# Two attention tiles kept in an empty weight buffer, and one attention tile and one operand sum moved to a later place

## The chip, the core and the metric

The kernel runs on one core of one Trainium2 chip. A core has five engines with a program of their own each: PE (TensorE) multiplies matrices into PSUM banks, DVE (VectorE) and ACT (ScalarE) work element by element, POOL (GpSimd) does the same out of SBUF only, and SP issues DMA transfers in the order of its own queue. An engine takes its instructions strictly in order, so a waiting instruction holds all that stand behind it. The metric is the device time of one execution in microseconds (us): the median of three runs is 307.73 us.

## The reference, cut to what matters

The first half is a linear attention (8 batches, 8 heads, 576 positions, 64 numbers per head), the second a gated feed-forward layer over all 4608 rows.

```python
r = np.maximum(x, 0.0)                     # phi, for q and k
phi = concatenate([r * cos, r * sin])      # 128 numbers per head and position
kv  = einsum('bhsf,bhsd->bhfd', k_p, v);  z = sum(k_p)
x   = (q_p @ kv) / (q_p @ z + 1e-6)        # per head; rows become (4608, 512)
out = (gelu(x @ w_gate) * (x @ w_val)) @ w_out    # d_ff = 1536
```

## The kernel before, in words

**Two ways of cutting the rows.** Attention goes by batch: batch b has five tiles of 128 rows (t = 0 to 4; of tile 4 only the last 64 rows are new). The feed-forward layer goes by block: nine blocks of 512 rows. Batch 2 begins at row 1152, so its tile 3 (rows 1536 to 1663) and its tile 4 (1664 to 1727) are the first 192 columns of block 3. Batch 3's tiles 0 and 1 and half of tile 2 are the rest of block 3; the other half of tile 2, tile 3 and tile 4 belong to block 4.

**One attention tile** (`nm_unit`, L310): eight small matmuls on PE (L312, 65 columns each) fill two PSUM banks, 6 and 7 unless told otherwise; DVE adds the epsilon (L323, `den`), takes the reciprocal (L324, `rec`) and multiplies (L325) into a tile `x_sb` in SBUF. The pool of `x_sb` has four buffers (`xsp`, L54), handed out in turn. Later `turn_x` (L376) has SP issue a transposing DMA per piece (L379) from `x_sb` into `xT` of the block; a buffer of `x_sb` can be written again once the DMAs that read it have landed.

**One block of the feed-forward layer.** Units 0 to 11 each make 128 of the 1536 columns. `gv_unit` (L421) makes one unit with plain matmuls (L431), a Gelu on ACT (L440, into one of two `gel` buffers) and a product on DVE (L443, into `hT`). From block 2 on some units are made in pairs by a seven-product scheme for two-by-two matrices (class `Pair`, L644; matmuls L655), which needs sums of weights, of `xT` (`x_sum`, L623, on POOL, into `fs`) and, for the output product, of `hT` (`h_sum`, L520, into `sm`, DVE or POOL). The helpers of a pair are p1 (copy L674 on ACT), p5 (copy L678), p6 (add L682 on DVE), p2 (Gelu L687), p3 (Gelu L691), p7 (add L695, product L696 on DVE) and p4 (product L700 on DVE). `product` (L539, matmuls L548, adds L561, copies L566) makes the output of the block before.

**Order.** Nothing is scheduled automatically: the order of the calls is the order of each engine's program. Block 2 (`block2`, L1017) makes half units 8 to 11, unit 4, pair (0, 1), unit 5, pair (2, 3), unit 6 and unit 7; `rest(jt)`, called once for each place jt, holds what else is done there: the attention of batch 3 (dictionary `tiles`, L1021; `turn_x` one place later), the products and sums of block 1 (`o_step`), the scaling of q and k of batch 4 (`early`, L1012, ACT and POOL), loads, and casts of v. Block 2's unit 7 puts its value half into bank 6 (L1065). From block 3 on `step` (L705) calls `numerators` (L1080) for the attention: at the start of a block it stands between p1 and p5 of the first pair, and there takes tile 4 of batch n. Its guard `b > 3` leaves out batch 3, whose tile 4 is in block 2's `tiles`. `kv_unit` of batch n + 1 (L265, matmuls L271) writes banks 6 and 7 in the next place but one.

**The empty place.** `wx` (L108) holds the sums S1, S2 and S4 of the weight columns 1024 to 1279, [128, 3, 2, 256] bf16. They are computed on POOL in block 3 (L1100, `w_sum`); up to there nothing reads or writes `wx`. One third of it is as large as one `x_sb` tile.

**The sum.** `SUMS` (L901) says at which place which sum of `hT` is made. For block 2's `o_step`, entry `9: "8"` is S4 of block 1's second half, a DVE instruction (L530, 128x768 bf16); product 3, which reads it, comes at place 11.

Of the kernel before, what the change touches and what calls it, by code (L numbers as in the profile page):

```python
# [10 lines left out]
BF16 = mybir.dt.bfloat16  # L11
# [5 lines left out]
def kernel(  # L17
# [15 lines left out]
    B, H, S, D = q.shape  # L33
# [20 lines left out]
    xsp = ctx.enter_context(tc.tile_pool(name="xsp", bufs=4))  # L54
# [11 lines left out]
    def bank(i):  # L66
        return ps[:, i]
# [40 lines left out]
    wx = weights.tile([128, 3, CT // 2, WX - WJ], BF16)  # L108
# [99 lines left out]
    def cast_v(b, m0, m1, copy, j0=0, j1=R):  # L208
        copy(  # L209
            vx[:, m0:m1, j0:j1, 0:D],  # L210
            staged["v", b][:, m0:m1, j0 * D:j1 * D].rearrange("p m (j d) -> p m j d", d=D),
        )
# [8 lines left out]
    def turn_q(b):  # L221
        for i in range(2):
            nc.sync.dma_start_transpose(
                out=qt_tile(b)[:, i].rearrange("f m (j p) -> f (m j) p", p=64),
                in_=phi["q", b][64 * i:64 * i + 64].rearrange("p m j f -> p (m j f)"),
            )

    def q_cols(b, t, h):
        c0 = min(t * 128, S - 128)
        return qT[b][:, h % 2, h // 2, c0:c0 + 128]  # L230
# [34 lines left out]
    def kv_unit(b):  # L265
        kp = phi["k", b]
        for m in range(NP):
            for j in range(R):
                for i in range(2):
                    rr = slice(64 * i, 64 * i + 64)  # L270
                    nc.tensor.matmul(  # L271
                        bank(6 + i)[:, m * (D + 1):(m + 1) * (D + 1)],
                        lhsT=kp[rr, m, j, :],
                        rhs=vx[rr, m, j, :],
                        start=(j == 0),
                        stop=(j == R - 1),
                    )
        kv_sb[b] = attn2.tile([128, NP, 2, D + 1], BF16, name="kv_sb")
        for i in range(2):
            nc.scalar.copy(  # L280
                kv_sb[b][:, :, i, :],
                bank(6 + i)[:, 0:NP * (D + 1)].rearrange("p (m d) -> p m d", m=NP),
            )
# [26 lines left out]
    def nm_unit(b, t, b0=6):  # L310
        for h in range(H):
            nc.tensor.matmul(  # L312
                bank(b0 + h // 4)[:, (h % 4) * (D + 1):(h % 4 + 1) * (D + 1)],
                lhsT=q_cols(b, t, h),
                rhs=kv_sb[b][:, h // 2, h % 2, :],
                start=True,
                stop=True,
            )
        nm = ps[:, b0:b0 + 2, 0:4 * (D + 1)].rearrange("p g (h d) -> p g h d", h=4)
        den = attn2.tile([128, 2, 4], FP32, name="den")  # L320
        rec = attn2.tile([128, 2, 4], FP32, name="rec")
        x = xsp.tile([128, 2, 4, D], BF16, name="x_sb")
        nc.vector.tensor_scalar_add(den, nm[:, :, :, D], EPS)  # L323
        nc.vector.reciprocal(rec, den)  # L324
        nc.vector.tensor_tensor(  # L325
            x,
            nm[:, :, :, 0:D],
            rec[:, :, :, None].to_broadcast([128, 2, 4, D]),
            op=ALU.mult,
        )  # L330
        xs[b, t] = x.rearrange("p g h d -> p (g h d)")
# [44 lines left out]
    def turn_x(b, t):  # L376
        x = xs.pop((b, t))
        for blk, c, o, m in pieces(b, t):
            nc.sync.dma_start_transpose(  # L379
                out=xT_block(blk)[:, :, c:c + m], in_=x[o:o + m, :]  # L380
            )
# [241 lines left out]
    def x_sum(n, i, eng=nc.gpsimd):  # L623
        if n not in xb:
            xt = xT[n]
            own = fs[:, (1 - n % 2) * 2 * BLK:(2 - n % 2) * 2 * BLK].bitcast(BF16)
            xb[n] = {
                "B11": xt[:, 0:CP, 0:256], "B12": xt[:, 0:CP, 256:512],
                "B21": xt[:, CP:CT, 0:256], "B22": xt[:, CP:CT, 256:512],
                "T": own.rearrange("p (i c n) -> p i c n", i=4, c=CP),  # L630
            }
        b = xb[n]
        x, y = (("B12", "B11"), ("B22", "T1"), ("B22", "B12"), ("B21", "T2"))[i]
        b[f"T{i + 1}"] = b["T"][:, i]
        eng.tensor_tensor(b[f"T{i + 1}"], b[x], b[y], op=ALU.subtract)  # L635
# [166 lines left out]
    prep("q", 0, 0, (6, 7))  # L802
    dummies(1, 1)
    nm_unit(0, 2, 4)
    turn_x_pe(0, 1, 7, act_copy)
    turn_j(0, 0, 2, (6, 7), 2, act_copy)
    turn_j(0, 2, 4, (6, 7), 3, dve_copy)
    gv_tile(0)
    nm_unit(0, 3, 6)
    gv_done(0)  # L810
    turn_x_pe(0, 2, 4, act_copy)
# [74 lines left out]
    def js(a, b):  # L886
# [12 lines left out]
        (5, 0): [(7, "q", 5, R), (7, "k", 5, R), (7, "v")],  # L899
    }  # L900
    SUMS = {  # L901
        2: {0: "1", 1: "2", 2: "34", 3: "567", 9: "8"},
        8: {i: str(i + 1) for i in range(8)},
    }
    for n in range(3, 8):
# [13 lines left out]
    def more(n, jt):  # L919
        for what in MORE.get((n, jt), ()):  # L920
            if len(what) == 3:
                w_sum(*what, eng=nc.gpsimd)
            else:
                x_sum(*what)
# [5 lines left out]
    def o_step(n, jt):  # L930
        p, u = divmod(jt, 6)
        for i in ((1, 2), (5,), (6,), (7,), (4,), (3,))[u]:
            product(n - 1, p, i, ps[:, 4, 0:CH], ps[:, 5, 0:CH], ps[:, 4, CH:C])
        for i in map(int, SUMS[n].get(jt, "")):
            eng = nc.gpsimd if n > 2 or jt == 3 else nc.vector
            h_sum(n - 1, i // 5, f"S{(i - 1) % 4 + 1}", eng=eng)
        if jt % 3 == 1:
            flush()

    def start_loads(n, jt):  # L940
        for b, name, *part in LOADS.get((n, jt), ()):
            if len(part) == 1:
                load(nc.sync, name, b, part[0], part[0] + 2)
            elif part:
                load(nc.sync, name, b, 0, NP, *part)
            else:
                for m in (0, 2):
                    load(nc.sync, name, b, m, m + 2)

    def scale(b, name, sines_, cosines):  # L950
        for j in sines_:
            prep(name, b, 1, (j,), eng=nc.scalar)
        for j in cosines:
            prep(name, b, 0, (j,))
# [57 lines left out]
    def early(jt):  # L1012
        for what in EARLY.get(jt, "").split():
            part = "cs".index(what[0])
            prep_both(4, part, int(what[1]), nc.scalar if part or jt > 8 else nc.gpsimd)

    def block2():  # L1017
        b, n = 3, 2
        o_step(n, 0)

        tiles = {4: 0, 5: 1, 6: 2, 7: 3, 10: 4}  # L1021

        def rest(jt):
            if jt - 1 in tiles:
                turn_x(b, tiles[jt - 1])
            if 0 < jt < JT - 1:
                o_step(n, jt)
            if jt in tiles:
                nm_unit(b, tiles[jt])
            if jt + JT in SCALE:  # L1030
                scale(*SCALE[jt + JT])
            if jt in (1, 2):
                cast_v(b, 2 * jt - 2, 2 * jt, act_copy)
            if jt == 3:
                kv_unit(b)
            early(jt)
            if jt == 1:
                turn_x(2, 3)
                turn_x(2, 4)
            start_loads(n, jt)  # L1040
            if jt == 2:
                for i in range(4):
                    x_sum(n, i)
            more(n, jt)
            if jt in (9, 10):
                m = 2 * (jt - 9)
                cast_v(4, m, m + 2, nc.gpsimd.tensor_copy)

        def rests(*jts):
            return [lambda jt=jt: rest(jt) for jt in jts]  # L1050

        turn[0] = 1
        for jt in range(4):
            for i in range(2):
                half, unit = divmod(2 * jt + i, 4)
                gv_unit(n, unit + 8, half * HALF, HALF)
                if jt == i == 0:
                    nm_unit(2, 4)
                    turn_q(3)
            rest(jt)  # L1060
        gv_unit(n, 4, to=(2, 3))
        rest(4)
        step(Pair(n, 0, 0, 2, range(5, 8)), None, *rests(5, 6, 7), std=5, to=1)
        step(Pair(n, 1, 2, 0, range(8, 11)), None, *rests(8, 9, 10), std=6, to=1)
        gv_unit(n, 7, to=(0, 6))  # L1065
        rest(11)
# [13 lines left out]
    def numerators(n, jt):  # L1080
        b, t = n + 1, {6: 0, 8: 1, 10: 2, 11: 3, 0: 4}.get(jt)
        if jt == 0:
            b = n
        if t is not None and b > 3:
            nm_unit(b, t)
            turns.append((b, t))

# [44 lines left out]
    turn[0] = 1  # L1132
    block1()
    block2()

    old, places = None, (0, 1, 2)
    for n in range(3, NB):
        jt = 0
        for T in range(JT // 2):
# [7 lines left out]
            jt = jts.stop  # L1147
# [17 lines left out]
    for what in (  # L1165
# [3 lines left out]
        if isinstance(what, str):  # L1169
            p = "ST".index(what[0])  # L1170
# [33 lines left out]
```

## Time and profile before

| | us |
|---|---|
| median of three runs (lowest, highest) | 307.73 (307.56, 307.85) |
| the profiled execution's own time | 307.25 |
| its span, first to last instruction | 305.5 |
| around the span | 1.75 |
| PE busy, of the span | 294.7 (96%) |
| DVE, ACT, POOL busy | 227.8, 203.9, 175.3 |
| granted clock of PE, mean | 0.997 |

The profile comes from one execution. Its times count from the first instruction. "Idle before, releaser" is the time in which the engine waited ahead of an instruction and what ended that wait. The starts of one group of matmuls and the next tell how fast PE goes: it starts a new group while the results of the last are still on their way, so a group's own duration is longer than the step to the next.

### The profile page before, as it was taken

What the parts mean: (1) busy time and instruction counts of PE and PEld (TensorE: products, weight loads), DVE (VectorE), ACT (ScalarE), POOL (GpSimd) and SP (SyncE); (2) the same over time, 40 slices, a digit from 0 to 9 for tenths busy, and PEclk for the clock granted to TensorE, in tenths of its full rate; (3) what the DMA queues carried; (4) which work ended last, traced back from release to release, by engine and by line L of the source; (5) the groups of instructions that cost most, each with busy time, mean ns of one, the idle gap of its engine ahead of it and who ended that gap; (6) DMA issues with size and microseconds to landing.
All of it is one profiled execution on the core that took longest, in us unless ns stands there. A gap on an engine that the chain in (4) does not pass through costs nothing.

```text
span 305.5 us, 8095 instructions
## 1 busy us (share of the span) xinstructions
PE 294.7 (96%) x3113; PEld 231.2 (76%) x3131; DVE 227.8 (75%) x497; ACT 203.9 (67%) x403; POOL 175.3 (57%) x147
## 2 busy tenths in 40 slices
PE   7899999999999899999999999999999999999993
PEld 2574455745788658888888888888898988888882
DVE  5866995998976675779677967796678785766782
ACT  7865593997574688869586958695655556555630
POOL 6675450000029999955955595669935965397310
PEclk9999999999999999999999999999999999999998
DMA  7999999989799997998999699918832321303045
GB/s 271 252 178 220 337 293 394 298 164 226 164 185 225 247 314 154 187 281 235 127 167 344 199 138 220 281 30 138 135 67 54 69 46 34 71 3 70 2 86 121
DMA packets 73175, 53.68 MB, mean 176 GB/s; under 512 B 45392, under 2 KB 62544, under 8 KB 73136
## 3 DMA queue, kind: packets, MB, share of 16 engines
q1 hardware_dynamic: 63360, 41.17, 59.2%
q0 software_dynamic: 9696, 11.93, 17.0%
q8 instruction: 24, 0.39, 0.6%
q14 instruction: 15, 0.12, 0.2%
q10 hardware_dynamic: 80, 0.07, 0.1%
HBM read 37.75 MB, written 9.44 MB: 154 GB/s over the span
## 4 chain that ended last, share of the span: by engine, by line
PE 75%; DMA 7%; issue 6%; DVE 5%; ACT 4%; POOL 1%; SPq 0%; POOLq 0%; DVEq 0%; ACTq 0%
PE ps L655 32%; PE ps L548 19%; PE ps L431 13%; PE ps L464 3%; DMA xT<-x_sb 3%; PE ps L271 2%; DMA st<-in_v_dram 2%; PE ps L312 2%; DMA wv_sb<-in_moe_w_val_dram 2%; DVE hT L443 1%; ACT gel L440 1%; POOL st L530 1%; ACT phis L178 1%; PE ps L402 1%; DVE x_sb L325 1%
## 5 line engine op out<-in xcount | busy, mean ns | idle before, releaser
L530 POOL TENSOR_TENSOR sm<-hT 128x768 bf16<-128x768 bf16 x26 | 42.7, 1643 | 17.7 <-PE ps L655 8.0
L635 POOL TENSOR_TENSOR fs<-xT 128x512 bf16<-128x512 bf16 x14 | 16.2, 1155 | 56.8 <-ACT vx L209 43.6
L655 PE MATMUL ps<-fs,ws 128*128 128x256 bf16 x312 | 44.4, 273 | 0.0
L655 PEld LDWEIGHTS <-ws 128*128 128x128 bf16 x416 | 39.5, 98 | 5.7 <-ACT ps L674 0.3
L695 DVE TENSOR_TENSOR ps<-fs,ps 128x512 f32<-128x512 f32 x35 | 24.3, 695 | 24.9 <-PE ps L655 23.1
L655 PE MATMUL ps<-xT,wg_sb 128*128 128x256 bf16 x280 | 42.0, 272 | 0.2 <-ACT gel L440 0.2
L431 PE MATMUL ps<-xT,wv_sb 128*128 128x512 bf16 (+1 forms) x167 | 37.9, 348 | 0.1
L431 PE MATMUL ps<-xT,wg_sb 128*128 128x512 bf16 (+1 forms) x155 | 36.8, 346 | 0.7
L548 PEld LDWEIGHTS <-sm 128*128 128x128 bf16 x336 | 32.3, 98 | 3.8
L687 ACT ACTIVATE gel<-ps 128x512 f32<-128x512 f32 x35 | 20.8, 594 | 19.5 <-PE ps L655 19.5
L561 DVE TENSOR_TENSOR o_sb<-sm,ps 128x256 f32<-128x256 f32 x56 | 23.4, 418 | 11.6 <-ACT sm L566 9.7
L655 PEld LDWEIGHTS <-wg_sb 128*128 128x128 bf16 x280 | 27.3, 98 | 5.5 <-issue 0.5
L678 ACT COPY fs<-ps 128x512 f32<-128x512 f32 x35 | 20.6, 588 | 16.2 <-DVE ps L695 16.2
L443 DVE TENSOR_TENSOR hT<-gel,ps 128x512 bf16<-128x512 f32 (+1 forms) x42 | 25.3, 606 | 8.1 <-PE ps L431 5.6
L440 ACT ACTIVATE gel<-ps 128x512 f32<-128x512 f32 (+1 forms) x42 | 22.3, 538 | 13.1 <-PE ps L431 10.7
L548 PEld LDWEIGHTS <-hT 128*128 128x128 bf16 x288 | 28.0, 98 | 3.8 <-issue 0.2
L325 DVE TENSOR_TENSOR x_sb<-ps,rec 128x512 bf16<-128x512 f32 x38 | 26.3, 691 | 3.0 <-DMA xT<-x_sb 1.5
L696 DVE TENSOR_TENSOR hT<-gel,ps 128x512 bf16<-128x512 f32 x35 | 24.1, 687 | 3.3
L691 ACT ACTIVATE gel<-ps 128x512 f32<-128x512 f32 x35 | 21.0, 599 | 8.2 <-PE ps L655 6.9
L431 PEld LDWEIGHTS <-wv_sb 128*128 128x128 bf16 x168 | 16.3, 98 | 12.9 <-issue 0.3
L530 POOL TENSOR_TENSOR sm<-hT,sm 128x768 bf16<-128x768 bf16 x12 | 19.7, 1644 | 11.0 <-PE ps L548 11.0
L192 ACT ACTIVATE phis<-st,sin_t 128x512 bf16<-128x512 f32 x36 | 25.6, 721 | 0.0
(134 smaller groups left out, 636.2 us busy)
## 6 DMA issues: line engine op xcount, KB each, us to landing
out_dram<-o_sb SPq DMA_DIRECT2D x69, 128.0 KB, 2.5
st<-in_v_dram SPq DMA_DIRECT2D x10, 576.0 KB, 6.7
st<-in_q_dram SPq DMA_DIRECT2D x5, 640.0 KB, 5.5
st<-in_q_dram SPq DMA_DIRECT2D x5, 512.0 KB, 5.0
st<-in_k_dram SPq DMA_DIRECT2D x4, 640.0 KB, 6.1
st<-in_k_dram SPq DMA_DIRECT2D x4, 576.0 KB, 4.6
st<-in_q_dram POOLq DMA_DIRECT2D x4, 576.0 KB, 12.1
st<-in_k_dram SPq DMA_DIRECT2D x4, 512.0 KB, 5.4
```

Source lines behind the costliest of these rows:

```text
L192: nc.scalar.activation(o, i, AF.Relu, scale=tab[:, j:j + 1])
L325: nc.vector.tensor_tensor(x, nm[:, :, :, 0:D], rec[:, :, :, None].to_broadcast([128, 2, 4, D]), op=ALU.mult,)
L431: nc.tensor.matmul(bank(to[g])[:, 0:w], lhsT=wt[:, ct, js], rhs=xt[:, ct, c0:c0 + w], start=(ct == 0), stop=(ct == CT - 1),)
L440: nc.scalar.activation(gel[:, 0:w], bank(to[0])[:, 0:w], AF.Gelu)
L443: nc.vector.tensor_mul(hT[n][:, jt, c0:c0 + w], gel[:, 0:w], bank(to[1])[:, 0:w])
L530: eng.tensor_tensor(a[name][:, j0:j1], a[x][:, j0:j1], a[y][:, j0:j1], op=op)
L548: nc.tensor.matmul(at, lhsT=hs.setdefault(key, h_parts(n, p))[a][:, j], rhs=ts[b][:, j], start=(j == 0 and i in ((1, 2, 4, 5), (1, 4, 5))[ ...
L561: nc.vector.tensor_tensor(o, got[key, k], x, op=op)
L655: nc.tensor.matmul(to[:, 256 * half:256 * half + 256], lhsT=w_part(a, j * 128, (j + 1) * 128)[:, ct], rhs=xb[self.n][b][:, ct], start=(hal ...
L691: nc.scalar.activation(gel1, bank(MIX), AF.Gelu)
L695: nc.vector.tensor_tensor(bank(val), self.m5, self.sum, op=ALU.add)
L696: nc.vector.tensor_tensor(self.h(1), both(gel1), both(bank(val)), op=ALU.mult)
```

## The change

Three edits. The tiles 3 and 4 of batch 2 are written to the first two thirds of `wx` instead of two `x_sb` buffers, and transposed from there; so the order in which buffers of `x_sb` are handed out skips these two. Tile 4 of batch 3 leaves block 2 (place 10) and is attended by `numerators` at the start of block 3, as the later batches' tile 4 is; its `turn_x` follows in the same place of block 3. Sum S4 of block 1's second half is made at place 10 instead of 9. The changed file has three lines more, so later lines stand 3 higher there.

```diff
         den = attn2.tile([128, 2, 4], FP32, name="den")
         rec = attn2.tile([128, 2, 4], FP32, name="rec")
-        x = xsp.tile([128, 2, 4, D], BF16, name="x_sb")
+        if (b, t) in ((2, 3), (2, 4)):
+            x = wx[:, t - 3].rearrange("p c (h d) -> p c h d", d=D)
+        else:
+            x = xsp.tile([128, 2, 4, D], BF16, name="x_sb")
...
-        2: {0: "1", 1: "2", 2: "34", 3: "567", 9: "8"},
+        2: {0: "1", 1: "2", 2: "34", 3: "567", 10: "8"},
...
-        tiles = {4: 0, 5: 1, 6: 2, 7: 3, 10: 4}
+        tiles = {4: 0, 5: 1, 6: 2, 7: 3}
...
         if jt == 0:
             b = n
-        if t is not None and b > 3:
+        if t is not None and b > 3 - (jt == 0):
             nm_unit(b, t)
```

## The prediction

> **What bounds the kernel now.** I read the busy shares first, then the chain that ended last, the waits, and the timeline of 92 to 118 us engine by engine. PE is busy 96% of the span, and from 112.8 us on the chain is almost wholly PE: what PE gains before that stays gained, unless something that does not move along catches it. Before that the chain leaves PE for a transposing DMA, and one wait in the list of waits belongs to it:
>
> ```profile
> 92.65 7.72 DMA xT<-x_sb
> ```
>
> ```profile
> DVE x_sb L325 <- DMA xT<-x_sb: 1.5, 1, 1.5
> ```
>
> SP issued that DMA at 92.65, for batch 2's tiles 3 and 4. By the hand-out order of the four `x_sb` buffers, batch 3's tile 2 takes the buffer of batch 2's tile 3; so its L325 waits for that landing, with DVE's whole queue behind it. DVE's timeline:
>
> ```profile
> 98.74 0.20 DVE L324 RECIPROCAL rec<-den 128x8 f32<-128x8 f32 x1
> 100.46 0.69 DVE L325 TENSOR_TENSOR x_sb<-ps,rec 128x512 bf16<-128x512 f32 x1 [1.51 <-DMA xT<-x_sb]
> 101.06 0.69 DVE L695 TENSOR_TENSOR ps<-fs,ps 128x512 f32<-128x512 f32 x1
> ...
> 108.66 0.70 DVE L695 TENSOR_TENSOR ps<-fs,ps 128x512 f32<-128x512 f32 x1 [0.22 <-ACT gel L691]
> ...
> 110.00 0.41 DVE L561 TENSOR_TENSOR o_sb<-sm,ps 128x256 f32<-128x256 f32 x1
> ...
> 110.76 0.69 DVE L325 TENSOR_TENSOR x_sb<-ps,rec 128x512 bf16<-128x512 f32 x1
> 111.37 0.68 DVE L700 TENSOR_TENSOR hT<-gel,ps 128x512 bf16<-128x512 f32 x1
> ```
>
> The L325 of 110.76 is batch 3's tile 4, the one that moves; L700 stands behind it. What PE loses is read from its own timeline (brackets: idle before, releaser):
>
> ```profile
> 99.59 0.82 PE L548 MATMUL ps<-wo_sb,sm 128*128 128x256 bf16 x6
> 101.20 0.42 PE L312 MATMUL ps<-kv_sb,qT 128*128 128x65 bf16 x8 [0.79 <-DVE x_sb L325]
> 101.80 0.60 PE L655 MATMUL ps<-fs,wv_sb 128*128 128x256 bf16 x4 [0.19 <-DVE ps L695]
> ...
> 103.97 0.82 PE L548 MATMUL ps<-T,sm 128*128 128x256 bf16 x6
> 104.81 0.60 PE L655 MATMUL ps<-fs,ws 128*128 128x256 bf16 x4
> ...
> 108.73 0.42 PE L312 MATMUL ps<-kv_sb,qT 128*128 128x65 bf16 x8
> 109.41 0.60 PE L655 MATMUL ps<-fs,wv_sb 128*128 128x256 bf16 x4 [0.26 <-DVE ps L695]
> ...
> 111.57 1.03 PE L431 MATMUL ps<-xT,wv_sb 128*128 128x512 bf16 x4
> 112.81 0.60 PE L655 MATMUL ps<-xT,wg_sb 128*128 128x256 bf16 x4 [0.21 <-ACT gel L440]
> 113.24 0.60 PE L655 MATMUL ps<-fs,ws 128*128 128x256 bf16 x4
> 113.68 0.82 PE L548 MATMUL ps<-wo_sb,sm 128*128 128x256 bf16 x6
> 114.52 0.61 PE L655 MATMUL ps<-fs,ws 128*128 128x256 bf16 x4
> ```
>
> Where nothing waits, the next group starts 0.44 after four matmuls of 256 columns (112.81 to 113.24), 0.66 after six, 0.86 after four of 512, 0.26 after eight of 65 (the chain's steps). Taking these steps off, PE's holes are 0.95 before 101.20, 0.34 before 101.80, 0.18 before 104.81, 0.42 before 109.41, 0.38 before 112.81 and 0.18 before 114.52: **2.45 us** in all. After 115 PE goes without a hole up to 122.
>
> **Part 1, the two tiles in `wx`.** No instruction is added: the same L325 (0.69) and the same transposes, from another place. `wx` is written again by POOL at 120.35 at the earliest, long after the landing at 100.37. Batch 3's tiles 0 to 3 now take the buffers of (1,4), (2,0), (2,1), (2,2), whose DMAs SP issued between 72 and 81 and which landed within 8.1 us, so none waits. L325 starts at 98.98 (0.24 after L324's start, as L324 and L325 of tile 4 stand at 110.52 and 110.76) instead of 100.46, and DVE is 1.48 earlier: L695 99.58, L696 100.30, L700 101.95. PE is ready for L312 at 99.59 + 0.66 = 100.25 and need not wait, nor for L695 (ends 100.28); so the holes of 0.95 and 0.34 go. ACT, idle before 104.19 while its copy L674 waited for L700, starts at 102.71, also 1.48 earlier, and the hole of 0.18 goes. Then **what is late next is ACT**: from 104.19 to 110.94 it works without a pause, so its Gelu L691, and with it the L695 of 108.66, can move by 1.48 and no more: to 107.18, ending 107.88.
>
> **Part 2, tile 4 of batch 3.** Its eight matmuls (0.26) leave the place before the L655 of 109.41. PE is now ready there at 107.27 and waits for L695 until 107.93: a hole of 0.66 in place of 0.42. DVE loses den, rec and x before L700, 111.37 - 110.33 = 1.04. After that PE runs units 6 and 7: 107.93 + 0.44 + 3 x 0.86 = 110.95, where block 3's first L655 (p1) begins; it began at 112.81. The Gelu L440 that releases it needs L700 (part 3: 110.08) and unit 7's gate (110.26), and ends at about 110.9: hole 0.
>
> Now the eight matmuls come behind p1, at 110.95 + 0.44 = 111.39. They write banks 6 and 7, and unit 7's value half lies in bank 6 until DVE's product L443 has read it. **That is a new wait.** Unit 7's last matmuls begin at 110.09 and end 1.03 later at 111.12; L443 starts 0.1 later (as one did at 92.99) and takes 0.68, so L312 starts at about 111.95: a hole of 0.56. Before, no such wait is in the trace; its bounds are 0 (L443 done in time) and the 0.95 of the nearest row, L312 behind L325 at 101.20. I take 0.56, because both its ends come from rows. All of PE stands behind it, p5 first. The DVE trio then runs at about 112.4 to 113.5, where DVE has nothing ready (before, it idled 1.06 ahead of 114.54), and ends before `kv_unit` wants banks 6 and 7 at 115.5. The hole of 0.18 before 114.52 goes: the copy L674 that releases it ends at 112.6, PE arrives at 113.3. SP's order is unchanged; the tile's transpose goes out at 113.5 instead of 112.08, its landing feeds only block 4, and the next issue, the qT transposes, waits for ACT's last scaling anyway (ends 115.2, was 116.8).
>
> **Part 3, the sum S4.** It leaves 107.89, where DVE had 0.22 to wait after it, and goes between L561 and L700: 0.55. So L700 starts at 111.37 - 1.48 - 1.04 + 0.55 = 109.40, ending 110.08. Cost nothing, because unit 7's gate (110.26) comes later; without that cover it would delay L440 by up to 0.55. Product 3, which reads it, is at 112.6. On POOL it meets another `x_sum`: the one beside it took 1.48 instead of 1.15, and POOL stays ahead: sum T1 is done at 107.9 and wanted at 112.2, S1 of block 2 at 115.5 and wanted at 118.6.
>
> **The sum.** Old holes 2.45, new ones 0.66 + 0.56 = 1.22; gain 1.2 us. At 116.81 (`kv_unit`) PE is at 115.6, and everything behind follows it. The profiled execution took 307.25 (span 305.5 and 1.75 around it) and would take 306.0; it is 0.5 below the median of 307.73, from which the same gain gives **306.5**.
>
> A rule against the change. The row first: batch 2's tile 3 landed 7.72 us after its issue, beside loads, and DVE waited. The Trainium skill ("DMA: Bandwidth & Descriptors", Latency and other measured facts) gives DMA transposes 261 GB/s; by that figure an estimate for the 131 KB of this tile is 0.5 us, its buffer is free long before 98.98, part 1 is worth nothing and the sum is that of the fourth rival below. I go by the trace.
>
> **Rivals.**
> - *The bank-6 wait is absent or hidden* (L443 quicker than worked out): gain 1.22 + 0.56 = 1.8, time 305.9. Against it: PE's end and L443 are both fixed by PE's own pace.
> - *Caught later*: the second qT transpose of batch 4, issued at 120.51, lands 7.0 to 7.8 later, at 127.5 to 128.3; L312 uses it at 128.64, which becomes 127.4. If the transposes do not move along, PE waits 0.1 to 0.9 there and the gain is 0.3 to 1.1: about 307.2. For the move speaks ACT's 115.2.
> - *Slower*: the same place, if the transposes are served one after another behind the moved tile's. That tile leaves 1.4 later; if the qT pair lands 1.4 later as well (128.9 to 129.7), PE waits 1.5 to 2.3 at 127.4, more than the gain: net loss 0.3 to 1.1, about 308.4. It decides from a landing later than 128.64. Against it: SP is free from 113.32 to 116.84 before.
> - *The change does not do what it says*: L325 is held at 100.46 by something else. Then only part 2 acts: holes 0.95 + 0.34 + 0.18 stay, 0.42 grows to 0.68, and 0.38 and 0.18 give way to 0.56: 2.7 against 2.45, time 308.0. Against it: the row names the DMA, and the buffer order agrees.
>
> **How the numbers follow.** Measurement can tell about 0.2% (0.6 us) from no change. Forecast 306.5 (306.0 to 307.0): 0.60; no bank wait 305.9: 0.10; caught later 307.2: 0.14; not what it says 308.0: 0.06; slower 308.4: 0.10. The range leaves out the last two: 305.7 to 307.6. Faster: 0.60 + 0.10 + under half of caught later = 0.74; same: the rest of that and 0.06, 0.15; slower: 0.10, and 0.01 for a slower end of the fourth rival: 0.11.
>
> **What would show it.** Right: L325 of batch 3's tile 2 without a wait; L700 behind it near 102; L312 in block 3's start with an idle of some 0.5 put down to DVE's L443; `kv_unit` near 115.6 instead of 116.81; the same distance of 1.2 at every later block. Wrong: L325 still waiting at 100.4; L312 near 127.4 waiting for a DMA; a POOL wait at block 3's sums; later blocks that win the 1.2 back or lose more.

## The result, and the profile after

The changed kernel takes 306.62 us (median of 13 runs, 305.54 to 307.75) against 307.73 (13 runs, 306.57 to 308.73): ratio 0.9963, 95% interval 0.9945 to 0.9981. The forecast was 306.5. The profiled execution took 305.86, with a span of 304.1 (before: 307.25 and 305.5; forecast: 306.0).

The chain of work that ended last, by engine, in the changed kernel:

```profile
PE 79%; DVE 6%; issue 5%; DMA 4%; ACT 2%; POOL 1%; SPq 0%; POOLq 0%; DVEq 0%; ACTq 0%
```

Before it read PE 75%, DMA 7%: the transposing DMA of 7.72 us has left the chain. DVE's timeline of the changed kernel (line numbers are 3 higher than before) shows why:

```profile
98.49 0.20 DVE L327 RECIPROCAL rec<-den 128x8 f32<-128x8 f32 x1
98.73 0.69 DVE L328 TENSOR_TENSOR x_sb<-ps,rec 128x512 bf16<-128x512 f32 x1
99.34 0.69 DVE L698 TENSOR_TENSOR ps<-fs,ps 128x512 f32<-128x512 f32 x1
...
108.59 0.60 DVE L533 TENSOR_TENSOR sm<-hT,sm 128x768 bf16<-128x768 bf16 x1
109.12 0.67 DVE L703 TENSOR_TENSOR hT<-gel,ps 128x512 bf16<-128x512 f32 x1
```

L328 of batch 3's tile 2 follows its reciprocal by 0.24, without a bracket: no wait. PE's timeline of the same execution:

```profile
99.35 0.82 PE L551 MATMUL ps<-wo_sb,sm 128*128 128x256 bf16 x6
100.00 0.42 PE L312 MATMUL ps<-kv_sb,qT 128*128 128x65 bf16 x8
100.26 0.60 PE L658 MATMUL ps<-fs,wv_sb 128*128 128x256 bf16 x4
...
102.44 0.82 PE L551 MATMUL ps<-T,sm 128*128 128x256 bf16 x6
103.09 0.60 PE L658 MATMUL ps<-fs,ws 128*128 128x256 bf16 x4
...
106.36 0.82 PE L551 MATMUL ps<-T,hT 128*128 128x256 bf16 x6
107.68 0.60 PE L658 MATMUL ps<-fs,wv_sb 128*128 128x256 bf16 x4 [0.50 <-DVE ps L698]
...
110.74 0.60 PE L658 MATMUL ps<-xT,wg_sb 128*128 128x256 bf16 x4
111.72 0.42 PE L312 MATMUL ps<-kv_sb,qT 128*128 128x65 bf16 x8 [0.38 <-DVE hT L446]
111.97 0.60 PE L658 MATMUL ps<-fs,ws 128*128 128x256 bf16 x4
...
115.34 1.33 PE L271 MATMUL ps<-vx,phis 64*128 64x65 bf16 x72
```

The groups of 100.00, 100.26 and 103.09 begin one step (0.65, 0.26, 0.65) after the group before, where holes of 0.95, 0.34 and 0.18 were; and two brackets that are left. One is the old wait for L695 (now L698), grown to a hole of 107.68 - 106.36 - 0.66 = 0.66; the other is new, tile 4's matmuls behind DVE's product of unit 7, a hole of 111.72 - 110.74 - 0.44 = 0.54.

**A finer measure.** Executions of one kernel differ by 2 us and more, and most of that arises early: the first `kv_unit` began anywhere from 46.98 to 48.91 in the profiles of this study, and from one `kv_unit` to the next they mostly agree to 0.03. From the first `kv_unit` to block 2's, a stretch in which the edits change only where two tiles are kept, it is 41.95 to 41.97 in all eleven profiles. So the experiments are read by D, the distance from block 2's `kv_unit` (L271) to block 3's: 116.81 - 89.72 = 27.09 before, 115.34 - 89.47 = 25.87 after, 1.22 less. All later distances are 30.65 or 30.66 in both, so what is won here is kept. Each D comes from one profiled execution; where a chance event fell into it, the text says so.

### The profile page after: what moved, and what is told of

The parts are those of the page before. It is cut to its first block, busy times and chain, and to the rows that moved or that the text cites. A ratio compares the mean times of both kernels' runs of the same rounds, so it can differ in the third digit from the quotient of the medians.

```text
span 304.1 us, 8112 instructions
## 1 busy us (share of the span) xinstructions
PE 294.9 (97%) x3131; PEld 231.1 (76%) x3131; DVE 227.4 (75%) x497; ACT 203.8 (67%) x403; POOL 173.3 (57%) x147
## 4 chain that ended last, share of the span: by engine, by line
PE 79%; DVE 6%; issue 5%; DMA 4%; ACT 2%; POOL 1%; SPq 0%; POOLq 0%; DVEq 0%; ACTq 0%
PE ps L658 33%; PE ps L551 20%; PE ps L434 15%; PE ps L467 3%; PE ps L312 3%; PE ps L271 3%; DMA st<-in_v_dram 2%; DMA wv_sb<-in_moe_w_val_dram 2%; DVE hT L446 2%; DVE phis L180 1%; POOL st L533 1%; PE ps L405 1%; DVE x_sb L328 1%; PE ps L234 1%; DVE ps L698 1%
## 5 line engine op out<-in xcount | busy, mean ns | idle before, releaser
L658 PE MATMUL ps<-fs,ws 128*128 128x256 bf16 x312 | 44.4, 273 | 0.0
L658 PEld LDWEIGHTS <-ws 128*128 128x128 bf16 x416 | 39.5, 98 | 5.2
L698 DVE TENSOR_TENSOR ps<-fs,ps 128x512 f32<-128x512 f32 x35 | 24.3, 695 | 25.3 <-PE ps L658 23.1
L658 PE MATMUL ps<-xT,wg_sb 128*128 128x256 bf16 x280 | 42.0, 272 | 0.0
L434 PE MATMUL ps<-xT,wg_sb 128*128 128x512 bf16 (+1 forms) x168 | 38.0, 349 | 0.0
L658 PEld LDWEIGHTS <-wg_sb 128*128 128x128 bf16 x280 | 27.3, 98 | 5.1 <-issue 0.2
L328 DVE TENSOR_TENSOR x_sb<-ps,rec 128x512 bf16<-128x512 f32 x36 | 24.9, 691 | 1.2
```

Source lines behind the costliest of these rows:

```text
L328: nc.vector.tensor_tensor(x, nm[:, :, :, 0:D], rec[:, :, :, None].to_broadcast([128, 2, 4, D]), op=ALU.mult,)
L434: nc.tensor.matmul(bank(to[g])[:, 0:w], lhsT=wt[:, ct, js], rhs=xt[:, ct, c0:c0 + w], start=(ct == 0), stop=(ct == CT - 1),)
L658: nc.tensor.matmul(to[:, 256 * half:256 * half + 256], lhsT=w_part(a, j * 128, (j + 1) * 128)[:, ct], rhs=xb[self.n][b][:, ct], start=(hal ...
L698: nc.vector.tensor_tensor(bank(val), self.m5, self.sum, op=ALU.add)
```

## The experiments

The theory is that of the prediction: the buffer wait is what was lost, ACT is what is late next, and tile 4's move brings a new wait on bank 6. The main rival is that tile 4's move brings a share of the gain. Each expectation was on record before its run. Ratios are against the kernel before, measured again beside each set of runs (medians 307.89 for e1 to e4, 307.73 for e7 to e10, 307.92 for e11), with 95% intervals. The medians tell kernels with part 1 from those without it, and little that is finer: the intervals of all the table's kernels with part 1 overlap or touch that of the changed kernel, 0.9945 to 0.9981. What is finer rests on D and on the rows.

| run | D, us | median, us | ratio |
|---|---|---|---|
| e1, part 1 alone | 25.62 | 306.65 | 0.9958 (0.9933 to 0.9983) |
| e2, parts 2 and 3 alone | 27.75 | 308.30 | 1.0009 (0.9988 to 1.0030) |
| e3, sum S4 at its old place | 25.88 | 306.84 | 0.9958 (0.9938 to 0.9978) |
| e4, unit 7 in bank 2 | 25.95 | 306.27 | 0.9951 (0.9931 to 0.9970) |
| e7, e4 with S4 at its old place | 25.33 | 305.76 | 0.9945 (0.9919 to 0.9971) |
| e9, part 2 alone | 28.11 | 308.19 | 1.0017 (0.9990 to 1.0044) |
| e10, one tile in wx | 25.88 | 306.34 | 0.9961 (0.9942 to 0.9979) |
| e11, e7 and ACT's order | 25.02 | 305.26 | 0.9909 (0.9873 to 0.9945) |

**e1: part 1 alone.** To the kernel before:

```diff
-        x = xsp.tile([128, 2, 4, D], BF16, name="x_sb")
+        if (b, t) in ((2, 3), (2, 4)):
+            x = wx[:, t - 3].rearrange("p c (h d) -> p c h d", d=D)
+        else:
+            x = xsp.tile([128, 2, 4, D], BF16, name="x_sb")
```

> Part 1 alone: batch 2's two tiles in wx, tile 4 of batch 3 and sum S4 at their old places. Measure: the distance D from kv_unit's first matmul in block 2 to the one in block 3, which leaves out what happened earlier; 27.09 us in the kernel before, 25.87 in the changed one. Theory (the buffer wait is the whole gain, part 2 gives a little back): the holes 0.95, 0.34 and 0.18 go, 0.42, 0.38 and 0.18 stay or shift with ACT, so D = 27.09 - 1.47 = 25.6, shorter than with all three parts, and the time is 1.5 below the kernel before. Rival (taking tile 4 off DVE's way to L700 is worth something of its own, and the new bank wait costs less than it brings): D lies above 25.87, at 26.2 or more.

D = 25.62, as the theory had it, and shorter than with all three parts. PE's timeline of this run keeps these two brackets:

```profile
107.17 0.60 PE L658 MATMUL ps<-fs,wv_sb 128*128 128x256 bf16 x4 [0.25 <-DVE ps L698]
110.56 0.60 PE L658 MATMUL ps<-xT,wg_sb 128*128 128x256 bf16 x4 [0.21 <-ACT gel L443]
```

They are the waits before 109.41 and 112.81 of the kernel before, where the brackets read 0.26 and 0.21: everything behind the buffer wait moved 1.47 forward as one piece. So part 1 is more than the whole gain, and parts 2 and 3 give back 0.25. By the medians e1 and the changed kernel can't be told apart; D tells them, and three profiles with the changed kernel's holes (its own, e3's and e10's) have a D of 25.87 or 25.88.

**e2: parts 2 and 3 without part 1.** To the changed kernel: the lines above undone.

> Parts 2 and 3 without part 1: the two tiles stay in x_sb buffers. Theory: DVE still stands about 1.5 us for the landing at batch 3's tile 2; PE keeps the holes 0.95, 0.34 and 0.18, the 0.42 grows to 0.68 and a bank-6 wait of 0.56 takes the place of 0.38 and 0.18: D = 27.09 + 0.26 = 27.35, the time 0.3 above the kernel before, not to be told from it. Rival (part 2 brings part of the gain): D below 26.8, a time 0.3 or more below.

D = 27.75: a loss, as the theory said and the rival did not, but 0.40 more than I had worked out. DVE's row of sum S4, and POOL's row beside it:

```profile
110.58 1.49 DVE L530 TENSOR_TENSOR sm<-hT,sm 128x768 bf16<-128x768 bf16 x1
```

```profile
110.50 1.15 POOL L635 TENSOR_TENSOR fs<-xT,fs 128x512 bf16<-128x512 bf16 x1
```

The sum took 1.49 instead of 0.55. It began just after POOL's `x_sum` T4 and ended 0.42 after it; L700 stood behind it, and Gelu L440 and block 3's first matmuls behind that (bracket there 0.59, before 0.21). By the rows PE lost 0.75 before block 3's first group and 0.29 before tile 4's, 1.04 where 0.56 was worked out, and 0.13 less at the buffer wait.

**e3: sum S4 back at place 9.** To the changed kernel:

```diff
-        2: {0: "1", 1: "2", 2: "34", 3: "567", 10: "8"},
+        2: {0: "1", 1: "2", 2: "34", 3: "567", 9: "8"},
```

> The changed kernel with sum S4 back at its old place 9. Theory: the sum is hidden at either place (behind ACT's Gelu there, under unit 7's gate here): D = 25.87 within 0.1 and the same time as the changed kernel. Rival (the sum at its new place delays L700 and through it L440 and block 3's first matmul): D shorter by 0.2 to 0.55.

D = 25.88: part 3 is hidden at both places, at these lengths of the sum: 0.55 at place 9, 0.60 in the changed kernel.

**e4: unit 7's value half in bank 2.** To the changed kernel:

```diff
-        gv_unit(n, 7, to=(0, 6))
+        gv_unit(n, 7, to=(0, 2))
```

> The changed kernel with one more edit: block 2's unit 7 puts its value half into bank 2, free by then, instead of bank 6. Theory (the hole ahead of tile 4's matmuls is bank 6, held until DVE's product of unit 7): the hole of 0.54 us before L312 in block 3's start goes, nothing else takes its place, D = 25.87 - 0.54 = 25.3, the time 1.8 below the kernel before. Rival (what comes next is as late: p5's operand, the copy of p1 on ACT, or batch 4's scaling ahead of kv_unit): the hole moves to the next group and D stays within 0.2 of 25.87.

D = 25.95, so by the number the rival holds, though none of the three things that it names was late. The bracket before tile 4's matmuls is gone, so bank 6 was what they waited for; but unit 7's value matmuls now wait:

```profile
111.00 1.02 PE L434 MATMUL ps<-xT,wv_sb 128*128 128x512 bf16 x4 [0.24 <-DVE hT L703]
```

L703 reads bank 2, and it stood behind sum S4, which took 0.99 here. That hole is 111.00 - 109.74 - 0.86 = 0.40; another 0.24 was lost at 93.64, where batch 3's first tile met a late piece of qT (its group took 0.66, not 0.42). So "free by then" was wrong.

**e7: bank 2, and S4 at place 9.** Both diffs above.

> The changed kernel with unit 7's value half in bank 2 and sum S4 back at place 9. In the run with bank 2 alone the hole before tile 4's matmuls went, but unit 7's value matmuls waited 0.40 for L703, which reads bank 2 and stood behind sum S4; the sum took 0.99 us there, not 0.55. Theory (bank 2 is free in time once the sum is off L703's way): no hole at unit 7 nor at tile 4, D = 25.87 - 0.54 = 25.33, give or take 0.25 for a late qT of batch 3. Rival (p1's copy, p5's operand or batch 4's scaling are as late): D stays above 25.6.

D = 25.33, the theory's number: with the sum off L703's way bank 2 is free in time, and tile 4's matmuls follow the group before them by one step. Between 97 and 115 us only one bracket is left:

```profile
107.83 0.60 PE L658 MATMUL ps<-fs,wv_sb 128*128 128x256 bf16 x4 [0.51 <-DVE ps L698]
...
110.88 0.60 PE L658 MATMUL ps<-xT,wg_sb 128*128 128x256 bf16 x4
111.32 0.42 PE L312 MATMUL ps<-kv_sb,qT 128*128 128x65 bf16 x8
```

**e8: ACT's order as well.** To e7:

```diff
-        2: {0: "1", 1: "2", 2: "34", 3: "567", 9: "8"},
+        2: {0: "1", 1: "2", 2: "34", 3: "567", 8: "8"},
...
-        7: "c0 c1 c2 c3 s0 s1 s2", 8: "s3 s4", 9: "c4", 10: "s5 c5 s6", 11: "c6 s7",
+        7: "c0 c1 c2 c3 s0 s1 s2", 8: "s3 s4", 10: "c4 s5 c5 s6", 11: "c6 s7",
```

> The same with sum S4 at place 8 and with one ACT scaling of batch 4 (c4, 0.62 us) moved from place 9, ahead of Gelu L694, to place 10, behind it. Theory (ACT bounds the hole of 0.66 before L658 at the end of pair (2, 3)): L694 and L698 start 0.62 earlier and the hole shrinks to under 0.1, D = 25.33 - 0.6 = 24.7, the time 2.4 below the kernel before. Rival 1 (not ACT but something behind it, DVE or PE's own product, ends that wait): D stays within 0.2 of the run with the sum at place 9. Rival 2 (the sum at place 8 is held by POOL's scalings, which run there, up to 1.98 each): L685 and PE behind it wait, D is 0.3 or more above 24.7.

I had overlooked that the load of batch 5's first q and k columns stands at place 9 and overwrites what c4 reads: c4 then works on batch 5's columns instead of batch 4's, and waits for them. ACT's timeline of this run:

```profile
106.00 0.63 ACT L694 ACTIVATE gel<-ps 128x512 f32<-128x512 f32 x1
106.90 0.60 ACT L443 ACTIVATE gel<-ps 128x512 f32<-128x512 f32 x1 [0.27 <-PE ps L434]
117.47 0.72 ACT L192 ACTIVATE phis<-st,cos_t 128x512 bf16<-128x512 f32 x1 [9.97 <-DMA st<-in_k_dram]
```

The median is 316.80 us, ratio 1.0300 (1.0266 to 1.0334), D = 37.65; that says nothing of the theory. What lies ahead of that wait does:

```profile
106.70 0.82 PE L551 MATMUL ps<-T,hT 128*128 128x256 bf16 x6
107.42 0.60 PE L658 MATMUL ps<-fs,wv_sb 128*128 128x256 bf16 x4
```

The hole at L658 is 107.42 - 106.70 - 0.66 = 0.06 instead of 0.66, so ACT was its cause. The sum's move is not: the hole was 0.68 with the sum ahead of L698 (e7) and 0.66 with the sum behind it (the changed kernel).

**e9: part 2 alone.** To the kernel before: only `tiles` and the guard of `numerators` as in the change.

> Part 2 alone: tile 4 of batch 3 at block 3's start, the two tiles in x_sb buffers, sum S4 at place 9. With parts 2 and 3 D was 27.75, 0.40 above what I had worked out, and sum S4 took 1.49 us beside POOL's sum T4. Theory (the 0.40 is the sum standing behind POOL, part 2 alone is as worked out): D = 27.35. Rival (the 0.40 belongs to tile 4's move or to the new bank wait): D = 27.7 or more again.

D = 28.11. D alone does not settle the question, because two disturbances fell into this run. PE waited for qT of batch 3 (bracket below; 94.57 - 93.34 - 0.26 = 0.97 in all), and sum S4, at its old place, met POOL's T2 and took 1.20, so that L695 held PE 1.02, where 0.68 was worked out. PE came later by the first, so the buffer wait cost it 0.40 instead of 0.95. Together 0.97 - 0.55 + 0.34 = 0.76, which is what D lies above 27.35.

```profile
94.33 0.40 PE L312 MATMUL ps<-kv_sb,qT 128*128 128x65 bf16 x7 [0.80 <-DMA qT<-phis]
```

What lies behind both is as worked out: from that L655 to `kv_unit` it is 117.80 - 110.14 = 7.66, against 116.81 - 109.41 = 7.40 before. The 0.26 more are tile 4's own eight matmuls, which now lie in this stretch; the waits there add up to the same, 0.04 + 0.53 against 0.38 + 0.18. So the 0.40 of e2 belongs neither to tile 4's move nor to the bank wait, and part 2 alone gains nothing here.

**e10: only tile 3 in wx.** To the changed kernel:

```diff
-        if (b, t) in ((2, 3), (2, 4)):
+        if (b, t) == (2, 3):
```

> The changed kernel with only batch 2's tile 3 in wx; its tile 4 takes an x_sb buffer, which batch 3's tile 3 then takes over. Theory (the loss is that the buffer was wanted before its DMA had landed, and batch 3's tile 3 comes 2.3 us after its tile 2): the DMA of batch 2's tile 4 has landed by about 100.4 and L328 of batch 3's tile 3 comes at 101.1 or later, so nothing waits and D = 25.87, give or take 0.1. Rival (that second DMA lands later than the first, and its buffer is wanted as urgently): L328 of batch 3's tile 3 waits and D is 26.2 or more.

D = 25.88, and L328 of batch 3's tile 3 does not wait:

```profile
101.19 0.20 DVE L327 RECIPROCAL rec<-den 128x8 f32<-128x8 f32 x1
101.43 0.69 DVE L328 TENSOR_TENSOR x_sb<-ps,rec 128x512 bf16<-128x512 f32 x1
```

The DMA of batch 2's tile 4 went out at 94.42 and landed 6.3 later, at 100.7. That of tile 3, now out of `wx`, still took 7.6 to land; no buffer of `x_sb` hangs on it any more. One buffer too few at one moment was the whole loss; the second tile in `wx` is not needed. That a fifth buffer of `x_sb` would do the same was not tried.

**e11: the load behind c4.** To e8:

```diff
-        (2, 9): [(5, "q", 0, 5), (5, "k", 0, 5)],
+        (2, 10): [(5, "q", 0, 5), (5, "k", 0, 5)],
```

> The changed kernel with unit 7's value half in bank 2, sum S4 at place 8, scaling c4 behind Gelu L694 at place 10, and the load of batch 5's first q and k columns at place 10 too, behind c4. In the run before, that load stayed at place 9, ahead of c4, so c4 waited for it 10 us. Theory (ACT bounded the hole of 0.66, as the first part of that run already showed: 0.06 there): D = 25.33 - 0.6 = 24.7, the time 2.4 below the kernel before. Rival (something that did not move along is late: POOL's sums of xT and hT, which start where they did, or the qT of batch 4): a hole of 0.2 or more at p5, p6 or the first L551 on a sum, or at L312 of batch 4, and D or the next distance is longer by it.

D = 25.02, the lowest D and the lowest median of the study, 305.26. PE's timeline:

```profile
93.52 0.72 PE L312 MATMUL ps<-kv_sb,qT 128*128 128x65 bf16 x8
...
107.05 0.82 PE L551 MATMUL ps<-T,hT 128*128 128x256 bf16 x6
107.76 0.60 PE L658 MATMUL ps<-fs,wv_sb 128*128 128x256 bf16 x4
```

The hole before L658 is 0.05, as the theory has it. The 0.3 missing to 24.7 is at 93.52: the group took 0.72 instead of 0.42, as in e4 and e9 where its qT came late. No later distance is longer.

## Why the prediction was right

Point by point; the changed execution was 0.25 ahead from before block 2's `kv_unit` on (89.47 against 89.72), so its times are given with 0.25 added.

- *Part 1.* L328 at 98.98 (said: 98.98), L703 101.95 (101.95), L677 on ACT 102.72 (102.71), L698 107.18 (107.18). The three holes went, and ACT is what is late next: e8 and e11 take one scaling of 0.62 from ahead of the Gelu, and the hole falls from 0.66 to 0.06 and 0.05. e1 shows that this part alone gives 1.47.
- *Part 2.* Block 3's first L658 at 110.99 (110.95), tile 4's matmuls at 111.97 (111.95), `kv_unit` at 115.59 (115.6). The new wait is bank 6: e4 takes it away, and e7 shows the 0.54 come out in D. That this part is a loss once part 1 is there was in the sum (0.42 + 0.38 + 0.18 became 0.66 + 0.56) but I did not say it; e1 does.
- *Part 3.* Right here: L703 at 109.37 (said: 109.40), and the Gelu behind it waited for unit 7's gate, as said. But half of the price was left out. The prediction put the sum down as 0.55 beside POOL and priced only what POOL loses. DVE is held as well: 0.60 here, but 0.99 in e4 and 1.49 in e2, where the "up to 0.55" that I set for a lost cover was too little. That the sum took only 0.60 in the changed kernel was luck: it started 0.19 before the end of a POOL instruction. Where POOL stands at that moment differs from run to run, because its scalings of batch 4 waited for a load: 1.14 in the changed kernel's profile, nothing in e2, 0.54 in e4. The prediction had left that wait out, and its T1, put at 107.9, was done at 109.03; it was wanted only at 112.2.
- *Rivals.* "Caught later" and "slower": the qT of batch 4 was issued 1.78 earlier (115.06 against 116.84; 0.25 of it from before), and the next distance is 30.65 as before. "Not what it says": L328 does not wait. "No bank wait" needs two further edits (e7), and then D is 1.76 less, as its 1.8 said. For "not what it says" I had worked out 308.0 from holes of 2.7, for which e2's expectation put D at 27.35; e2 had 27.75, and the step that failed there is the price of the sum.
- *The rule against the change.* By the estimate of 0.5 us, worked out from the 261 GB/s that the Trainium skill ("DMA: Bandwidth & Descriptors", Latency and other measured facts) gives for DMA transposes, part 1 would have been worth nothing; e1 gives it 1.47. The figure is a bandwidth, and what counted was the time from issue to landing, 7.72 in the kernel before. No run here shows what that time is made of.

## What to carry to other kernels

When a rotating buffer is wanted before its DMA has landed, look for an idle tile of the right size elsewhere, and first ask how many buffers are short: here it was one. After the wait is gone, follow each engine's row up to the first one without a pause; that engine (here ACT, 6.75 us of unbroken work) fixes how much arrives. A tile moved into the cover of a later stage brings its own waits, so try each part of a change alone: here one part gave back 0.25 of what another won.

## What the runs showed of the hardware that I had not expected

**A DVE sum was held by a two-input instruction on POOL.** Sum S4 reads two bf16 operands from SBUF. Alone it takes 0.55. Where it begins while POOL's `x_sum` (two SBUF operands, 1.15) runs, it ends 0.41 or 0.42 after that one's end, however early it began, and POOL's next instruction is stretched by 0.2 to 0.33. POOL's rows of the changed kernel, beside the sum of 108.59:

```profile
107.63 1.15 POOL L638 TENSOR_TENSOR fs<-xT 128x512 bf16<-128x512 bf16 x1
108.86 1.35 POOL L638 TENSOR_TENSOR fs<-xT,fs 128x512 bf16<-128x512 bf16 x1
```

| run | sum S4, start and us | POOL's instruction at its start, end | sum's end after it | POOL's next, us |
|---|---|---|---|---|
| after | 108.59, 0.60 | 108.78 | 0.41 | 1.35 |
| e10 | 108.94, 0.64 | 109.16 | 0.42 | 1.36 |
| e4 | 109.36, 0.99 | 109.94 | 0.41 | 1.47 |
| e9 | 108.28, 1.20 | 109.07 | 0.41 | 1.47 |
| e2 | 110.58, 1.49 | 111.65 | 0.42 | two casts, 2.57 for 2.24 |

The Trainium skill ("SBUF — State Buffer", Who interferes with whom) says that a DVE instruction with two SBUF inputs contends with a GpSimd instruction that reads SBUF, and that the order of issue decides which of them blocks. The table agrees for POOL's `x_sum`. For POOL's scalings (L194, one fp32 tile as input, 1.98 each) the runs do not: S4 began before the end of one in e1, e3, e7 and e11 and took 0.55, in e8 0.74. Which difference between the two POOL instructions matters no run here shows.

**The qT transposes of batch 3 have no slack.** L312 at about 93.5 met them late in e4, e9 and e11, by 0.24, 0.97 and 0.30; in all three its weight loads waited for the DMA into qT (0.27, 0.99 and 0.33). Nothing ahead of it differs from runs that met them in time (e1 and the changed kernel with e4 and e11, the kernel before with e9), so D can be longer by that much from one execution to the next.
